# Attention by whole chunks, float32 scores in two row halves of the array, and equal slices of four chunks

## The chip, the cores and the metric

One core of a Trainium2 chip runs the whole program. The metric is the device time of one execution in microseconds. The engines of the core are TensorE (PE in the profile; its weight loads are PEld), VectorE (DVE), ScalarE (ACT), GpSimd (POOL) and SyncE (SP), which here only issues transfers.

## The reference

Two parts follow each other. A decaying linear attention over 4 batches, 8 heads, 768 positions and 64 features gives `x`; a feed-forward layer with a squared ReLU gives the output. Inputs of attention are float32; the weights of the layer are float64.

```python
for b in range(nb):                       # blocks of 64 positions
    intra = np.einsum('bhic,bhjc->bhij', qb, kb) * Dmask[None]     # lam^(i-j), zero above the diagonal
    intra = np.einsum('bhij,bhjd->bhid', intra, vb)
    inter = np.einsum('bhid,bhde->bhie', qb * lam_pow[None], kv_state)
    out[:, :, sl] = intra + inter
    kv_state = lam_block[None, :, None, None] * kv_state + np.einsum('bhsd,bhse->bhde', kb * rev_pow[None], vb)
...
x = out.transpose(0, 2, 1, 3).reshape(3072, 512)
h = x @ w_in                              # 512 x 2048
r = np.maximum(h, 0.0)
return ((r * r) @ w_out).astype(np.float32)   # 2048 x 512
```

## The kernel before, in words

**Attention.** It works in chunks of 128 positions: 6 chunks for each batch, 24 in all, numbered t. Heads go in pairs that fill the 128 partitions, 4 pairs for a chunk. For a pair, `scores` multiplies k by q, where q of the two heads is laid out block-diagonally (`qbd`, 128 rows, 256 columns), so that one product gives both heads. `masked` multiplies the scores by the powers of the decay (`mask`) on VectorE. `products` adds three kinds of products: what the chunk adds to the state (from k and v), the values (from v and the masked scores), and, where a chunk is not the first of its batch, the state times q. The first two kinds use column halves of the array, one for each head of a pair; the third uses the whole array. `update` brings the state `kv` up to date on VectorE. `prep` multiplies k and q by powers of the decay on GpSimd, in place.

**Two forms of the scores.** Up to chunk 8 they are float32 products. From chunk 9 on (`T1`), `divide` splits q and k into two parts each (`qh`, `ql`, `kh`, `kl`, type float32r), and `scores2` adds three products for each pair; `attend2` then takes two pairs at a time.

**Feed-forward.** It also keeps each operand in two float32r parts and leaves out the product of the two low parts. Tokens go in slices of 5, 4, 4, 4, 4 and 3 chunks (`GS`). In a slice, unit f of 16 computes 128 of the 2048 hidden features (`hidden`, 12 products of 512 columns for four chunks), `relu` and `square` on ScalarE (and VectorE) and `rest` on VectorE make the squares' two parts `gh` and `gl`, and `project` adds 3 products for each chunk to that chunk's bank. On TensorE the order is hidden(f), then attention for chunks of the next slice, then project(f-1). The split of the next slice's input, `xh` and `xl`, is done at the end of a slice from `xt`, since `xh` and `xl` exist once.

**Conversion of the weights.** A piece of 512 columns of float64 is turned into float32 bit by bit: `first` (two operations on ScalarE), `clamp`, `shift`, `sign`, `rounded` (VectorE), `upper` (ScalarE, the high part) and `lower` (VectorE, the low part; on GpSimd for pieces 0 and 2). There are 32 pieces, 16 for each matrix. Two are done before the first slice, and unit f of slice 0 converts two more. `wload` issues a piece's load when a buffer comes free.

**What sets the order.** Each engine runs its instructions in the order in which the program issues them. Tiles come from pools with a fixed number of buffers, and a new tile waits until the last user of its buffer is done. Transfers are issued on SP in program order as well; an instruction there that waits for a buffer holds up those behind it. PSUM has 8 banks: 4 for `project`'s sums (`ps_acc`), 2 for `hidden` (`ps_h`), one each for `ps_x` and `ps_a`.

**Start.** The decays' powers are computed on VectorE from `lam`, written to memory (`zd`) and read back as `mask` and `qpow`. Attention of the first five chunks runs before the feed-forward part, two pairs a step.

Of the kernel before, what the change touches and what calls it, by code (L numbers as in the profile page):

```python
# [9 lines left out]
I32 = mybir.dt.int32  # L10
# [16 lines left out]
GS = (5, 4, 4, 4, 4, 3)     # attention chunks in a slice of the feed-forward part  # L27
G0 = GS[0]
T1 = G0 + GS[1]             # from this chunk on, scores are products of operands in two parts
N = 4 * C  # L30
NM = len(GS)

NST, NA = 4, 4              # tiles for raw and converted weights
# [3 lines left out]
TURNS = [[1]] + [[j for j in (2 * f + 2, 2 * f + 1) if j < 2 * NF] for f in range(1, NF)]  # L37

# Before the first slice, step k takes two pairs of a chunk, and beside them:
CONVERT = (4, 5, 6, 7, 7)   # steps that convert piece 2 further  # L40
FIRST, RAW, SPREAD, LOW0, LOW2 = 3, 3, 2, 5, 8
AHEAD = {1: (5,), 2: (6,), 3: (7,), 4: (8,), 5: (9,)}   # steps whose scores it computes
LA = 10                     # pairs whose scores come before step 0
WARM = 2, 2
PARTS = 1, 2                # parts of a unit's first products that go before the scores
# [3 lines left out]
def body(ctx: ExitStack, tc: tile.TileContext, qT, kT, kvq, lam, w, out):  # L49
# [32 lines left out]
    warm(WARM[0])  # L82

    loaded, tok = {}, {}
    banks = [0]

    def bank():             # the banks of ps_acc and the one of ps_x in turn
        banks[0] += 1
        if banks[0] % G0 == 0:
            return ps_x.tile([P, DM], F32, name="x")  # L90
        return ps_acc.tile([P, DM], F32, name="acc")

    rooms = [const.tile([P, 3 * DM], F32, name=f"kvq{j}") for j in range(2)]

    def room(t):
        return rooms[t] if t < 2 else lent[:, 0 : 3 * DM] if t == 2 else rooms[(t + 1) % 2]

    def qroom(t):
        if t == G0 - 1 and t not in extra:
            extra[t] = wk.tile([P, DM], F32, name="q4", tag="A", bufs=NA)  # L100
        return extra[t] if t == G0 - 1 else room(t)[:, 2 * DM :]

    extra = {}

    def load_qk(t):
        if T1 <= t < NT:
            k_ = io.tile([P, NPR, C], F32, name="kT_sb", bufs=1)
            nc.sync.dma_start(out=k_, in_=kT[t])
            loaded[t] = None, k_
        elif t < NT:  # L110
            if t < G0 and t % 2:
                q_, k_ = qbd[1], lent[:, 3 * DM : 4 * DM].rearrange("p (a b) -> p a b", a=NPR)
            else:
                q_, k_ = qbd[0], io.tile([P, NPR, C], F32, name="kT_sb", bufs=1) if t != 2 else None
            if t == 2:
                k_ = wk.tile([P, DM], F32, name="k2", tag="A", bufs=NA).rearrange("p (a b) -> p a b", a=NPR)
            if t == 3:
                load_q(t)
            nc.sync.dma_start(out=k_, in_=kT[t])
            if t in (1, 2):  # L120
                load_q(t)
            elif t not in (3, 4):
                for j in range(2):
                    r = slice(j * D, (j + 1) * D)
                    nc.sync.dma_start(out=q_[r, :, j, :], in_=qT[t, r])
            loaded[t] = q_, k_

    def load_q(t):
        nc.sync.dma_start(out=qroom(t), in_=kvq[t, :, 2 * DM :])

    def spread(t):
        x = qroom(t).rearrange("p (a b) -> p a b", a=NPR)
        for j in range(2):
            r = slice(j * D, (j + 1) * D)
            nc.scalar.copy(loaded[t][0][r, :, j, :], x[r])

    def load_v(t):
        if t < NT:
            x = room(t)
            n = 3 * DM if t >= G0 and t % NCB or t >= T1 else 2 * DM  # L140
            nc.sync.dma_start(out=x[:, 0:n], in_=kvq[t, :, 0:n])
            x = x[:, 0:DM], x[:, DM : 2 * DM], qroom(t)
            tok[t] = [y.rearrange("p (a b) -> p a b", b=z) for y, z in zip(x, (D, D, C))]

# [1 line left out]
    wih = const.tile([P, NF, KT * P], F32R, name="wih")  # L146
    wil = const.tile([P, NF, KT * P], F32R, name="wil")
    woh = const.tile([P, NF, DM], F32R, name="woh")
    wol = const.tile([P, NF, DM], F32R, name="wol")
    NW = 2 * NF  # L150
    order = [0, 2] + [j for x in TURNS for j in x]
    raw, cv, loads = {}, {}, iter(order)

    def wload(n=1):
        for _ in range(n):
            j = next(loads, None)
            if j is not None:
                raw[j] = wk.tile([P, DM], I64, name="raw", tag="st", bufs=NST)
                nc.sync.dma_start(out=raw[j], in_=w[j % 2, :, j // 2])
# [5 lines left out]
    def first(j):  # L165
        r = raw.pop(j).bitcast(U32).rearrange("p (n two) -> p n two", two=2)
        A = wk.tile([P, DM], U32, name="A", bufs=NA)
        nc.scalar.activation(A.bitcast(F32), r[:, :, 1].bitcast(F32), AF.Abs)  # L168
        nc.scalar.activation(r[:, :, 0], r[:, :, 0], AF.Copy, scale=2.0**-29)
        cv[j] = r[:, :, 0], r[:, :, 1], A  # L170

    def clamp(j):           # beyond float32's range: to zero and to infinity
        A = cv[j][2].bitcast(F32)
        nc.vector.tensor_scalar(
            out=A, in0=A, scalar1=2.0**-15, scalar2=float(LIM), op0=ALU.max, op1=ALU.min
        )

    def shift(j):
        A = cv[j][2]
        nc.vector.tensor_scalar(  # L180
            out=A, in0=A, scalar1=3, scalar2=0x3FFFFFFF,
            op0=ALU.logical_shift_left, op1=ALU.bitwise_and,
        )

    def sign(j):
        L, Hw, A = cv[j]
        nc.vector.scalar_tensor_tensor(
            out=A, in0=Hw, scalar=0xC0000000, in1=A, op0=ALU.bitwise_and, op1=ALU.bitwise_or
        )

    def rounded(j):
        L, Hw, A = cv[j]
        nc.vector.tensor_tensor(out=A, in0=A, in1=L, op=ALU.add)
        if j not in order[:2]:
            wload()

    def upper(j):
        nc.scalar.copy((wih, woh)[j % 2][:, j // 2], cv[j][2].bitcast(F32))

    def lower(j, eng=nc.vector):  # L200
        hi, lo = ((wih, wil), (woh, wol))[j % 2]
        eng.tensor_tensor(  # L202
            out=lo[:, j // 2], in0=cv.pop(j)[2].bitcast(F32), in1=hi[:, j // 2].bitcast(F32),
            op=ALU.subtract,
        )
# [538 lines left out]
```

## Time and profile before

| | |
|---|---|
| time, median of 3 runs | 655.0 us (654.37 to 655.11) |
| span of the profiled execution | 653.3 us |
| TensorE busy | 642.7 us (98%) |
| VectorE busy | 342.1 us (52%) |
| ScalarE busy | 247.7 us (38%) |
| GpSimd busy | 55.0 us (8%) |
| moved by DMA | 50.41 MB, mean 77 GB/s |

The profiled execution's own time is given by its span; what lies around it (launch and end) is only in the times of the runs. Busy times are sums over one execution, and an engine's instructions are pipelined, so that a TensorE that is 98% busy isn't 98% used. A row such as `L454 PE MATMUL h<-xh,wih 128*128 128x512 f32 x256 | 69.1, 391` says: line 454, TensorE, result tile and operands, the part of the array that is used, the shape, how often, the busy time in us and the mean of one in ns. In rows with times, the first number is the start in us from the beginning of the span, the second the duration in us, and what stands in brackets is the idle time ahead of it and what ended it. In a table of stretches, the columns are the stretch and its length, then the busy time of PE, PEld, DVE, ACT and POOL, the granted clock of TensorE, the share of DMA and GB/s.

### The profile page before, as it was taken

The numbers are of one execution on the slowest core, as the hardware profiler recorded it, in microseconds if no ns is written. First come the engines' busy times: TensorE is split into PE (matmuls) and PEld (weight loads), VectorE is DVE, ScalarE is ACT, GpSimd is POOL, SyncE is SP. The second block draws the span as 40 slices with busy tenths as digits, with TensorE's granted clock in tenths as the row PEclk, the third lists the DMA queues.
The fourth block names the chain that finished last, engine by engine and source line by source line (L and its number), as shares of the span: only waits on it lengthen the run. The fifth ranks groups of instructions, "written<-read, shape, count | busy, mean of one in ns | idle before, by whom it ended". The sixth has DMA issues, their size and how long they took to land.

```text
span 653.3 us, 9153 instructions
## 1 busy us (share of the span) xinstructions
PE 642.7 (98%) x3620; PEld 533.3 (82%) x3620; DVE 342.1 (52%) x669; ACT 247.7 (38%) x459; POOL 55.0 (8%) x58
## 2 busy tenths in 40 slices
PE   7989999999999999999999999999999999999997
PEld 3778888888888888888888888788888888889996
DVE  4998887887743433735344454254474452242222
ACT  3367776676522232523313333223153222242222
POOL 2520101001101100101001010011010100000000
PEclk9899999999999999999999999999999999999999
DMA  6854545451420201211101121022031000010001
GB/s 230 301 178 140 203 147 189 132 212 45 145 64 1 65 23 42 82 49 64 65 1 65 33 97 64 1 65 66 1 128 49 19 0 1 0 65 1 0 2 48
DMA packets 19963, 50.41 MB, mean 77 GB/s; under 512 B 1992, under 2 KB 6096, under 8 KB 19920
## 3 DMA queue, kind: packets, MB, share of 16 engines
q1 hardware_dynamic: 19920, 49.82, 22.7%
q8 instruction: 28, 0.46, 0.3%
q14 instruction: 15, 0.12, 0.1%
HBM read 43.52 MB, written 6.30 MB: 76 GB/s over the span
## 4 chain that ended last, share of the span: by engine, by line
PE 92%; DVE 4%; DMA 3%; issue 1%; ACT 0%; SPq 0%; DVEq 0%
PE h L454 40%; PE acc L493 13%; PE acc L498 13%; PE acc L494 13%; PE x L414 3%; PE att L336 3%; PE att L331 3%; PE att L326 2%; DMA raw<-in_w 1%; DVE kv L369 1%; PE att L298 1%; DVE a L314 1%; DMA zd<-pw 1%; DMA mask<-zd 1%; PE x L493 1%
## 5 line engine op out<-in xcount | busy, mean ns | idle before, releaser
L463 ACT ACTIVATE r<-h 128x512 f32<-128x512 f32 (+2 forms) x112 | 59.6, 535 | 314.6 <-PE h L454 314.6
L472 DVE TENSOR_TENSOR r<-r 128x512 f32<-128x512 f32 (+1 forms) x80 | 60.2, 753 | 165.8 <-ACT gh L468 165.2
L493 PE MATMUL acc<-woh,gh 128*128 128x512 f32 x368 | 146.6, 398 | 0.0
L498 PE MATMUL acc<-woh,gl 128*128 128x512 f32 x368 | 143.9, 391 | 0.0
L494 PE MATMUL acc<-wol,gh 128*128 128x512 f32 x368 | 143.6, 390 | 0.0
L454 PE MATMUL h<-xh,wih 128*128 128x512 f32 (+2 forms) x448 | 110.1, 367 | 0.0
L454 PE MATMUL h<-xl,wih 128*128 128x512 f32 (+2 forms) x448 | 107.2, 360 | 0.3 <-DVE xl L555 0.3
L454 PE MATMUL h<-xh,wil 128*128 128x512 f32 (+2 forms) x448 | 106.1, 358 | 0.1
L454 PEld LDWEIGHTS h<-xl,wih 128*128 128x128 f32 x448 | 79.9, 188 | 11.0 <-DVE xl L555 0.5
L454 PEld LDWEIGHTS h<-xh,wil 128*128 128x128 f32 x448 | 79.4, 188 | 10.4 <-DVE wil L202 0.4
L454 PEld LDWEIGHTS h<-xh,wih 128*128 128x128 f32 x448 | 78.3, 188 | 10.2
L498 PEld LDWEIGHTS acc<-woh,gl 128*128 128x128 f32 x368 | 69.0, 188 | 15.3
L493 PEld LDWEIGHTS acc<-woh,gh 128*128 128x128 f32 x368 | 69.2, 188 | 13.7 <-ACT r L463 0.5
L494 PEld LDWEIGHTS acc<-wol,gh 128*128 128x128 f32 x368 | 69.2, 188 | 13.5
L477 DVE TENSOR_TENSOR gl<-r,gh 128x512 fp32r<-128x512 f32 (+2 forms) x96 | 69.1, 720 | 10.7 <-ACT r L470 4.2
L369 DVE SCALAR_TENSOR_TENSOR kv<-kv,qpow,att 64x64 f32<-64x64 f32 x96 | 26.9, 280 | 72.2 <-ACT xt L433 64.9
L468 ACT ACTIVATE gh<-r 128x512 fp32r<-128x512 f32 (+2 forms) x96 | 61.0, 635 | 1.7
L276 POOL TENSOR_TENSOR kvq<-kvq,qpow 128x512 f32<-128x512 f32 x17 | 22.0, 1291 | 413.7 <-DVE ql L404 327.4
L421 DVE TENSOR_TENSOR a<-x,mask 128x512 f32<-128x512 f32 x30 | 20.7, 690 | 13.4 <-PE x L414 13.0
L331 PE MATMUL att<-a,kvq 128*64 128x128 f32 x304 | 25.0, 277 | 0.0
L168 ACT ACTIVATE A<-raw 128x512 f32<-128x512 f32 x32 | 21.3, 666 | 8.2 <-DMA raw<-in_w 8.2
L336 PE MATMUL att<-kvq,kv 128*128 128x128 f32 x128 | 24.4, 305 | 0.0
(123 smaller groups left out, 582.2 us busy)
## 6 DMA issues: line engine op xcount, KB each, us to landing
raw<-in_w SPq DMA_DIRECT2D x32, 512.0 KB, 5.0
kvq<-in_kvq SPq DMA_DIRECT2D x18, 768.0 KB, 4.3
out_x<-o SPq DMA_DIRECT2D x24, 256.0 KB, 2.3
kT_sb<-in_kT SPq DMA_DIRECT2D x21, 256.0 KB, 2.6
kvq<-in_kvq SPq DMA_DIRECT2D x5, 512.0 KB, 5.3
qbd<-in_qT SPq DMA_DIRECT2D x10, 128.0 KB, 3.1
lent<-in_kT SPq DMA_DIRECT2D x2, 256.0 KB, 3.0
kvq<-in_kvq SPq DMA_DIRECT2D x2, 256.0 KB, 4.5
```

The costliest lines, as they stand in the source:

```text
L276: (nc.vector if t == 1 else nc.gpsimd).tensor_tensor(out=qd, in0=qd, in1=qpow, op=ALU.mult)
L331: nc.tensor.matmul(o[e][r], vs[:, 2 * p + j, :], a[:, 2 * e + j, :], start=e == 0 and clear, stop=not t % NCB, skip_group_check=True,)
L336: nc.tensor.matmul(o[e], kv[:, p, :], qd[:, p, :], start=False, stop=True, skip_group_check=True,)
L369: nc.vector.scalar_tensor_tensor(out=d, in0=d, scalar=qpow[r, p, C - 1 : C], in1=u[r], op0=ALU.mult, op1=ALU.add)
L454: nc.tensor.matmul(h, wt[:, f, kt * P : (kt + 1) * P], x[:, kt, cs], start=k == 0, stop=k == 11)
L463: nc.scalar.activation(rr, h, AF.Relu)
L468: nc.scalar.activation(gh, r, AF.Square)
L472: nc.vector.tensor_tensor(out=r, in0=r, in1=r, op=ALU.mult)
L477: nc.vector.tensor_tensor(out=gl, in0=r, in1=gh.bitcast(F32), op=ALU.subtract)
L493: nc.tensor.matmul(accs[m][i], gh[:, cs], woh[:, f], start=f == 0, stop=False)
L494: nc.tensor.matmul(accs[m][i], gh[:, cs], wol[:, f], start=False, stop=False)
L498: nc.tensor.matmul(accs[m][i], gl[:, cs], woh[:, f], start=False, stop=end)
```

## The change

It is a new version of the program's body. Constants and the computation of the powers stay; the arithmetic of the feed-forward part stays. What differs:

- All six slices have four chunks. Four chunks of attention run before the first slice.
- Attention takes a whole chunk at a time, one chunk for four units: scores in the first of them, `masked` in the second, `attend` in the third. Scores are float32 products throughout. Each head's product uses 64 rows of the array, the two heads of a pair the two row halves, and they write to two banks. `qbd`, `divide` and `scores2` are gone; `ps_a` has two banks and `ps_x` is gone.
- The state times q uses column halves as well, 8 products. The state's decay is multiplied ahead on GpSimd (`decay`, into `kvd`), and VectorE adds with two instructions for each chunk in place of eight.
- `xh` and `xl` have two buffers each; `attend` writes the next slice's input split into them, from the PSUM bank.
- Weights are converted in 17 lots: the first and the last are one piece, the others two (`pieces`), with one instruction of 1024 columns for each step. `lower` runs on GpSimd for all of them. Unit f of slice 0 converts lot f+2. `raw` and `A` have two buffers.
- `square` works in the PSUM bank: relu, and both squares on ScalarE. `rest` reads the bank.
- Loads: q and k of a chunk by features, and k and v by tokens, each in a tile with two buffers. Chunks 2 and 3 use memory of `xh` and `xl`. At the start the loads of four chunks and of lots 0 and 1 are issued in a row on SP; the transfers of the powers go by ScalarE's queue.
- The output is staged in tiles that use `raw`'s buffers.

The diff, cut to its core:

```diff
-GS = (5, 4, 4, 4, 4, 3)     # attention chunks in a slice of the feed-forward part
...
+G = 4
+N = G * C
+NM = NT // G
+NLOT = NF + 1
...
+    def load_qk(t):
+        if t in (2, 3):
+            lent[t] = wk.tile([P, 2, KT * C, 2], F32, name=f"lent{t}", tag=("xh", "xl")[t - 2])
+            x = lent[t][:, 0].rearrange("p a b -> p (a b)")
+        else:
+            x = io.tile([P, 2 * DM], F32, name="qk_sb")
...
+    def pieces(u):
+        return slice(max(2 * u - 1, 0), min(2 * u + 1, 2 * NF))
...
+            raw[u] = wk.tile([P, n], I64, name="raw", tag="raw")
...
+    def first(u):
+        if u < NLOT:
+            r = raw.pop(u).bitcast(U32).rearrange("p (n two) -> p n two", two=2)
+            A = wk.tile([P, r.shape[1]], U32, name="A")
+            nc.scalar.activation(A.bitcast(F32), r[:, :, 1].bitcast(F32), AF.Abs)
+            nc.scalar.activation(r[:, :, 0], r[:, :, 0], AF.Copy, scale=2.0**-29)
...
+    def lower(u, eng):
+        eng.tensor_tensor(
+            out=flat(wl, u), in0=cv.pop(u)[2].bitcast(F32), in1=flat(wh, u).bitcast(F32),
+            op=ALU.subtract,
+        )
...
+    wload(0)
+    load_kv(0)
+    load_qk(2)
+    load_kv(1)
+    load_kv(2)
+    wload(1)
+    load_qk(3)
+    load_kv(3)
...
+    def scores(t, pool, name):
+        sc_of[t] = [pool.tile([P, DM], F32, name=name) for _ in range(2)]
+        k_, q_ = feat[t][:, 0], feat[t][:, 1]
+        for p in range(NPR):
+            for j, r in enumerate(rows):
+                nc.tensor.matmul(
+                    sc_of[t][j][:, p * C : (p + 1) * C], k_[r, p], q_[r, p],
+                    start=True, stop=True, skip_group_check=True,
+                )
...
+    def attend(t, pool, name):
...
+        for p, j, r in heads if c else []:
+            nc.tensor.matmul(
+                o[r, p * C : (p + 1) * C], kv[:, p, rows[j]], q_[:, p, :], start=False, stop=True,
+                skip_group_check=True,
+            )
+        if c < NCB - 1:
+            for j, r in enumerate(rows):
+                x = u[r, 0 : NPR * D].rearrange("p (a b) -> p a b", a=NPR)
+                d = kv[r, :, rows[j]]
+                if c:
+                    V.tensor_tensor(out=d, in0=kvd[r], in1=x, op=ALU.add)
+                else:
+                    V.tensor_copy(d, x)
+        xh, xl = xs_of[t // G]
+        cs = slice(t % G * C, (t % G + 1) * C)
+        o = o.rearrange("p (a b) -> p a b", a=KT)
+        nc.scalar.copy(xh[:, :, cs], o)
+        return lambda: V.tensor_tensor(
+            out=xl[:, :, cs], in0=o, in1=xh[:, :, cs].bitcast(F32), op=ALU.subtract
+        )
+
+    def decay(t):
+        if t % NCB < NCB - 2:
+            for j, r in enumerate(rows):
+                nc.gpsimd.tensor_tensor(
+                    out=kvd[r], in0=kv[r, :, rows[j]],
+                    in1=qpow[r, :, C - 1 : C].broadcast_to([D, NPR, D]), op=ALU.mult,
+                )
...
+    def square(h):
+        nc.scalar.activation(h, h, AF.Relu)
+        gh = wk.tile([P, N], F32R, name="gh")
+        nc.scalar.activation(gh, h, AF.Square)
+        nc.scalar.activation(h, h, AF.Square)
+        return gh
...
+    first(0)
+    for op in (clamp, shift, sign, rounded):
+        op(0)
+    upper(0)
+    first(1)
+    prep_k(0)
+    masked(0)
+    prep_k(1)
+    prep_q(1)
+    later = [[], [clamp, shift], [sign], [rounded]]
+    for t in range(G):
+        if t + 1 < G:
+            masked(t + 1)
+        if t + 2 < G:
+            scores(t + 2, ps_acc, "acc")
+        low = attend(t, *((ps_h, "h") if t % 2 else (ps_a, "att")))
+        low()
+        decay(t)
+        if t + 2 < G:
+            prep_k(t + 2)
+            prep_q(t + 2)
+        for op in later[t]:
+            op(1)
+        if t == 1:
+            lower(0, nc.gpsimd)
+    upper(1)
+    lower(1, nc.gpsimd)
+    wload(2)
+    first(2)
...
     for m in range(NM):
+        if m + 1 < NM:
+            new_x(m + 1)
         for f in range(NF):
+            u = f + 2 if m == 0 and f + 2 < NLOT else None
+            t = (m + 1) * G + f // 4
+            step = f % 4 if t < NT else None
+            h = hidden(m, f, *xs_of[m])
+            if step == 1:
+                masked(t)
+            if u is not None:
+                wload(u + 1)
+                for op in (clamp, shift, sign):
+                    op(u)
+            gh = square(h)
+            low = attend(t, ps_a, "att") if step == 2 else None
+            if u is not None:
+                rounded(u)
+                upper(u)
+                first(u + 1)
+            rest(m, f, h, gh)
+            if low:
+                low()
+                decay(t)
+                if t + 2 < NT:
+                    load_qk(t + 2)
+                    load_kv(t + 2)
+            if u is not None:
+                lower(u, nc.gpsimd)
             if prev is not None:
                 project(*prev)
             prev = (m, f)
+            if step == 0:
+                scores(t, ps_a, "att")
+                prep_k(t)
+                prep_q(t)
```

More of the change, by code (lines that the diff above doesn't have):

```diff
@@ L26 @@
 NF = DF // P
-GS = (5, 4, 4, 4, 4, 3)
[L28 to L45, printed above, removed]
+G = 4
+N = G * C
+NM = NT // G
+NLOT = NF + 1
 @with_exitstack
@@ L80, in warm @@
             nc.tensor.matmul(w_, kv[:, 0, :], kv.rearrange("p a b -> p (a b)"), start=True, stop=True)
[L82 to L103, printed above, removed]
-    def load_qk(t):
[L106 to L143, printed above, removed]
@@ L146, in body @@
[L146 to L159, printed above, removed]
@@ L165, in first @@
[L165 to L176, printed above, removed]
@@ new lines, in w_out, with wload @@
+    def w_out(f):
+        return 2 * f + 2 if f < NF - 1 else 2 * NF - 1
+    def pieces(u):
+        return slice(max(2 * u - 1, 0), min(2 * u + 1, 2 * NF))
+    raw, cv = {}, {}
+    def wload(u):
+        if u < NLOT:
+            x = pieces(u)
+            n = (x.stop - x.start) * DM
+            raw[u] = wk.tile([P, n], I64, name="raw", tag="raw")
+            for i, j in enumerate(range(x.start, x.stop)):
+                of = (1, j // 2 - 1) if j and j % 2 == 0 else (1, NF - 1) if j == 2 * NF - 1 else (0, (j + 1) // 2)
+                nc.sync.dma_start(out=raw[u][:, i * DM : (i + 1) * DM], in_=w[of[0], :, of[1]])
@@ L183, in shift, with sign, rounded, flat @@
         )
-    def sign(j):
-        L, Hw, A = cv[j]
-        nc.vector.scalar_tensor_tensor(
+    def sign(u):
+        L, Hw, A = cv[u]
+        V.scalar_tensor_tensor(
             out=A, in0=Hw, scalar=0xC0000000, in1=A, op0=ALU.bitwise_and, op1=ALU.bitwise_or
         )
[L191 to L201, printed above, removed]
+    def rounded(u):
+        L, Hw, A = cv[u]
+        V.tensor_tensor(out=A, in0=A, in1=L, op=ALU.add)
+    def flat(t, u):
+        return t[:, pieces(u)].rearrange("p a b -> p (a b)")
+    def upper(u):
+        nc.scalar.copy(flat(wh, u), cv[u][2].bitcast(F32))
+    def lower(u, eng):
         eng.tensor_tensor(
-            out=lo[:, j // 2], in0=cv.pop(j)[2].bitcast(F32), in1=hi[:, j // 2].bitcast(F32),
+            out=flat(wl, u), in0=cv.pop(u)[2].bitcast(F32), in1=flat(wh, u).bitcast(F32),
             op=ALU.subtract,
@@ L426, in attend2 @@
-    def attend2(i, xt, at):
-        t, p0 = divmod(i, NPR)
-        c = t % NCB
-        b = ps_a.tile([P, DM], F32, name="att")
-        o = b[:, 2 * C :].rearrange("p (e i) -> p e i", e=2)
-        us = [b[:, e * D : (e + 1) * D] for e in range(2)] if c < NCB - 1 else None
-        products(t, (p0, p0 + 1), lot["a"], [o[:, 0], o[:, 1]], us, us is None)
-        nc.scalar.copy(xt[:, p0 : p0 + 2, at : at + C], o)
-        for e in range(2) if us else []:
-            update(i + e, us[e])
-    g_of, accs = {}, {}
@@ L440, in parts @@
-    def parts(m):
-        n = GS[m] * C
-        k = -(-n // 512)
-        return [slice(j * n // k, (j + 1) * n // k) for j in range(k)]
-    def hidden(m, f, xh, xl, todo):
-        r = one.tile([P, GS[m] * C], F32, name="r")
-        for cs in parts(m):
-            h = ps_h.tile([P, cs.stop - cs.start], F32, name="h")
-            todo.append((r, r[:, cs], h))
-            k = 0
-            for wt, x in ((wih, xh), (wih, xl), (wil, xh)):
-                for kt in range(KT):
-                    nc.tensor.matmul(
-                        h, wt[:, f, kt * P : (kt + 1) * P], x[:, kt, cs], start=k == 0, stop=k == 11
-                    )
-                    k += 1
-                    if k % 3 == 0:
-                        yield
@@ L482, in project @@
         if f == 0:
-            if m == 0:
-                accs[m] = []
-                for _ in range(G0):
-                    accs[m].insert(0 if (banks[0] + 1) % G0 == 0 else len(accs[m]), bank())
-            else:
-                accs[m] = [ps_acc.tile([P, DM], F32, name="acc") for _ in range(GS[m])]
+            accs[m] = [ps_acc.tile([P, DM], F32, name="acc") for _ in range(G)]
         end = f == NF - 1
+        j = w_out(f)
         def high(i):
             cs = slice(i * C, (i + 1) * C)
-            nc.tensor.matmul(accs[m][i], gh[:, cs], woh[:, f], start=f == 0, stop=False)
@@ L522, in body @@
-    for i in range(2 * NPR, LA):
-        scores(i)
-    warm(WARM[1])
+        xs_of[m] = [wk.tile([P, KT, N], F32R, name=n, tag=n) for n in ("xh", "xl")]
+    new_x(0)
+    scores(0, ps_acc, "acc")
+    scores(1, ps_acc, "acc")
+    warm(2)
     for h, n in ((0, 4), (4, 4)):
-        nc.sync.dma_start(
+        nc.scalar.dma_start(
             out=mask[:, h : h + n],
@@ L529, in body @@
         )
-    load_v(1)
     for j in range(2):
-        nc.sync.dma_start(
-            out=qpow[j * D : (j + 1) * D],
+        nc.scalar.dma_start(
+            out=qpow[rows[j]],
             in_=bass.AP(zd.tensor, zd.offset + j * Z + C, [[0, D], [2 * Z, NPR], [1, C]]),
         )
-    load_qk(3)
-    load_v(2)
-    load_q(4)
-    load_qk(4)
-    wload()
     first(0)
-    for op in (clamp, shift, sign):
+    for op in (clamp, shift, sign, rounded):
         op(0)
-    rounded(0)
+    upper(0)
@@ L545, in body @@
+    first(1)
+    prep_k(0)
     masked(0)
-    upper(0)
-    prep(0)
-    more = []
-    for op in (clamp, shift, sign, rounded, upper):
-        more.append(lambda op=op: op(2))
-    late = []
-    def xpart(o, p, cs):
-        nc.scalar.copy(xh[:, p, cs], o)
-        late.append(lambda: nc.vector.tensor_tensor(
-            out=xl[:, p, cs], in0=o, in1=xh[:, p, cs].bitcast(F32), op=ALU.subtract
-        ))
-    todo = []
-    early = hidden(0, 0, xh, xl, todo)
-    for k in range(NE // 2):
-        i = 2 * k
-        t, p = divmod(i, NPR)
-        masked(i + 2)
-        while late:
-            late.pop()()
-        for _ in range(CONVERT.count(k)):
-            more.pop(0)()
-        o, us = attend(i)
-        for e in range(2):
-            update(i + e, us[e])
-        if k == 1:
-            prep(1)
-        if t == G0 - 1:
-            next(early)
-            next(early)
-        for j in AHEAD.get(k, ()):
-            scores(2 * j)
-            scores(2 * j + 1)
-        cs = slice(t * C, (t + 1) * C)
-        if t == G0 - 1:
-            xpart(o, slice(p, p + 2), cs)
-        elif p == 2:
-            xpart(o_of.pop(t), slice(0, NPR), cs)
-        if p == 2:
-            t = (3, 4, NT, 5, 6)[t]
-            if t == 3:
-                spread(t)
-                prep(2)
-            load_v(t)
-            prep(t)
-        if k == RAW:
-            wload(2)
-        if k == SPREAD:
-            spread(4)
-        if k == FIRST:
-            first(2)
-        if k == LOW0:
-            lower(0, nc.gpsimd)
-        if k == LOW2:
-            lower(2, nc.gpsimd)
@@ L602, in body @@
-    for op in late + more:
-        op()
-    queue = iter(order[2:])
-    for j in TURNS[0]:
-        first(next(queue))
-    def split(kt):
-        nc.scalar.copy(xs[0][:, kt], xt[:, kt])
-        nc.vector.tensor_tensor(
-            out=xs[1][:, kt], in0=xt[:, kt], in1=xs[0][:, kt].bitcast(F32), op=ALU.subtract
-        )
+    prep_k(1)
[15 more added lines that the diff above has]
+        if t == 1:
+            lower(0, nc.gpsimd)
@@ L614, in body @@
+    upper(1)
+    lower(1, nc.gpsimd)
+    wload(2)
+    first(2)
+    for t in (4, 5):
+        load_qk(t)
+        load_kv(t)
     prev = None
[L615 to L616 removed]
     for m in range(NM):
[L618 removed]
+        if m + 1 < NM:
+            new_x(m + 1)
         for f in range(NF):
[L620 to L677 removed]
```

344 lines of the change are left out of this document (89 added, 255 removed).

## The prediction

> **What bounds the kernel now.** I read the page's head first, then busy time in four stretches that I cut where the work changes: attention alone, slice 0, slices 1 to 4, slice 5.
>
> ```profile
> span 653.3 us, 9153 instructions
> PE 642.7 (98%) x3620; PEld 533.3 (82%) x3620; DVE 342.1 (52%) x669; ACT 247.7 (38%) x459; POOL 55.0 (8%) x58
> ...
> 0.00:35.30 35.30, 29.36 (x219) 19.70 (x220) 25.75 (x88) 11.63 (x19) 13.83 (x22) 0.95 0.78 260
> 35.30:166.00 130.70, 130.24 (x800) 113.05 (x799) 107.72 (x222) 91.68 (x177) 10.31 (x11) 1.00 0.47 157
> 166.00:579.40 413.40, 413.38 (x2257) 337.89 (x2256) 187.51 (x324) 125.58 (x230) 30.84 (x25) 1.00 0.14 45
> 579.40:653.30 73.90, 69.76 (x349) 62.66 (x347) 21.16 (x37) 18.81 (x37) 0.00 (x0) 0.99 0.07 26
> ```
>
> TensorE is the bound from 35.3 us on: it has no idle time in slices 1 to 4. But in slice 0 VectorE is busy for 107.72 of 130.70 us and ScalarE for 91.68, because the weights are converted there. That slice has little room on three engines at once. The chain of waits, in order of time, gives the unit prices (start, us, what):
>
> ```profile
> 10.91 4.03 DMA mask<-zd
> ...
> 59.11 3.52 PE h L454 x24
> 67.29 3.52 PE h L454 x24
> ...
> 179.98 2.72 PE h L454 x12
> 185.42 0.71 PE x L414 x6
> ...
> 193.11 2.72 PE h L454 x12
> ...
> 557.69 2.72 PE h L454 x12
> 563.13 2.72 PE h L454 x12
> ...
> 648.03 0.45 PE acc L498 x2
> ```
>
> Starts of `hidden` 557.69 and 563.13: a unit of four chunks without attention is 5.44 us. 179.98 to 193.11: two units with two pairs' attention are 13.13, so attention for two pairs is 13.13 - 10.88 = 2.25: split scores 0.71, the rest 1.54. A whole chunk costs 4.50. In slice 0 a unit of five chunks with one pair takes 67.29 - 59.11 = 8.18. After TensorE's last matmul (648.48) 4.8 us of copy and store remain.
>
> **The change, part by part: TensorE.** All slices have four chunks: 96 units of 5.44 are 522.2 us, fixed. Attention: the starts of weight loads inside one `attend2` are
>
> ```profile
> 175.68 0.31 PEld L326 LDWEIGHTS att<-kvq 128*64 128x64 f32 x8 [0.35 <-issue]
> 175.91 0.42 PEld L331 LDWEIGHTS att<-a,kvq 128*64 128x64 f32 x8
> 176.50 0.52 PEld L336 LDWEIGHTS att<-kvq,kv 128*128 128x128 f32 x4 [0.17 <-issue]
> L326 PEld LDWEIGHTS att<-kvq 128*64 128x64 f32 x240 | 9.9, 136 | 10.8 <-issue 10.2 <-POOL kvq L281 0.2 <-DVE A L180 0.2
> ```
>
> Each float32 product is two instructions. The array waits 0.35 where it goes from the whole array to column halves and 0.17 on the way back. A chunk at once has the products of two `attend2`, 3.08, less one entry (0.35) and, as the state's products now use column halves too, both returns (0.34): 2.4. The scores become 8 products on 64 rows each, 16 instructions, alternating between the row halves and two banks. No row shows row halves. Nearest is L331: 8 instructions of 128 columns in column halves, 0.42. Twice that is 0.85, plus entry 0.35 and exit 0.1: 1.3. Chunks that start a batch lack the state's products and those that end one the update (mean of -0.1 to -0.2). I take 3.6 per chunk where it was 4.5. Ends: 3.2 (no entry waits) and 4.45 (row halves one after the other, +0.85). Sixteen chunks stand beside slices 1 to 4: 57.6 us.
>
> Whether the weight loads allow this: eight loads of 64 columns span 0.31 with 136 ns for one, so they start 25 ns apart; sixteen of 128 columns would need 0.8, no more than the products. The Trainium skill, "TensorE: Matmul & The Clock Gate", section "LDWEIGHTS (loading the stationary operand)", counts columns over 1.2 per ns, and not rows, so a 64-row load saves nothing: by it sixteen loads take 1.71 us, and the sum would be 13.7 us higher. The eight loads above took less than that rule gives (0.43), so I do not follow it.
>
> **Conversion in slice 0.** Two pieces become one operation of 1024 columns, and `lower` moves from VectorE to GpSimd for all of them. Within a round everything is one ring: `upper(u)`, then `first(u+1)` behind it on ScalarE, then clamp, shift, sign and rounded on VectorE, then `upper(u+1)`. Before, two pieces were interleaved on each engine, and the ring hid under 8.18 us of TensorE. Its parts at 512 columns, and how they grow:
>
> ```profile
> 10.74 0.67 ACT L168 ACTIVATE A<-raw 128x512 f32<-128x512 f32 x1
> 11.45 0.43 DVE L174 TENSOR_SCALAR A<-A 128x512 f32<-128x512 f32 x1 [4.84 <-ACT A L168]
> 11.91 0.43 DVE L180 TENSOR_SCALAR A<-A 128x512 uint32<-128x512 uint32 x1
> 12.37 0.69 DVE L187 SCALAR_TENSOR_TENSOR A<-raw,A 128x512 uint32<-128x512 uint32 x1
> 13.21 0.69 DVE L193 CUSTOM_DVE_ANT_0 A<-raw,A 128x1024 uint16<-128x1024 uint16 x1
> 13.93 0.62 ACT L198 CAST wih<-A 128x512 fp32r<-128x512 f32 x1 [1.93 <-DVE A L193]
> L477 DVE TENSOR_TENSOR gl<-r,gh 128x640 fp32r<-128x640 f32 x16 | 13.2, 822 | 4.6 <-ACT r L470 4.2
> L477 DVE TENSOR_TENSOR gl<-r,gh 128x384 fp32r<-128x384 f32 x16 | 8.9, 559 | 1.6
> L468 ACT ACTIVATE gh<-r 128x640 fp32r<-128x640 f32 x16 | 11.9, 746 | 0.0
> L468 ACT ACTIVATE gh<-r 128x384 fp32r<-128x384 f32 x16 | 8.4, 526 | 0.5
> L202 POOL TENSOR_TENSOR wil<-A,wih 128x512 fp32r<-128x512 f32 x2 | 2.8, 1375 | 0.0
> L281 POOL TENSOR_TENSOR kvq<-kvq,mask 128x128 f32<-128x128 f32 x4 | 1.5, 402 | 11.5 <-DMA mask<-zd 11.5
> L281 POOL TENSOR_TENSOR kvq<-kvq,mask 128x512 f32<-128x512 f32 x18 | 20.9, 1162 | 4.8 <-DMA kvq<-in_kvq 4.8
> ```
>
> VectorE adds (822-559)/256 = 1.03 ns per column, half that in clamp and shift (next fence), ScalarE 0.86, GpSimd (1162-402)/384 = 1.98. At 1024 columns: upper 1.06, Abs 1.11, clamp 0.74, shift 0.74, sign 1.37, rounded 1.25 and two hand-overs of 0.04: 6.35 us. TensorE's mean in slice 0 is 5.44 + 3.6/4 = 6.34. So the ring would just not matter, if nothing held it. But `lower` on GpSimd runs right after `upper`, when clamp is next. What a GpSimd operation does to VectorE:
>
> ```profile
> 25.53 1.06 POOL L281 TENSOR_TENSOR kvq<-kvq,mask 128x512 f32<-128x512 f32 x1 [2.03 <-DMA kvq<-in_kvq]
> 25.57 0.68 DVE L555 TENSOR_TENSOR xl<-acc,xh 128x512 fp32r<-128x512 f32 x1
> 26.17 0.70 DVE L174 TENSOR_SCALAR A<-A 128x512 f32<-128x512 f32 x1
> 26.55 1.45 POOL L276 TENSOR_TENSOR q<-q,qpow 128x512 f32<-128x512 f32 x1
> ...
> 509.34 1.06 POOL L281 TENSOR_TENSOR kvq<-kvq,mask 128x512 f32<-128x512 f32 x1
> 509.71 1.24 DVE L472 TENSOR_TENSOR r<-r 128x512 f32<-128x512 f32 x1 [1.84 <-ACT gh L468]
> ```
>
> The clamp that began at 26.17 ended at 26.87, 0.28 after GpSimd's operation (26.59); the product at 509.71 ended at 510.95, 0.55 after GpSimd's (510.40). Both waited for its end. The subtraction at 25.57, which reads a PSUM bank and one SBUF operand, lost nothing. The Trainium skill, "SBUF — State Buffer", section "Who interferes with whom", says the same of a pair of ports that one instruction holds to its end; by that rule a 1024-column `lower` holds it throughout, which no row here shows at that length.
>
> `lower` at 1024 columns: 1.375 + 512 x 1.98 ns = 2.4 us (ends: 2.0, and 2.75 for twice the row). It starts 1.14 after `rounded` and ends at 3.53; clamp, which would have ended at 1.06+1.11+0.08+0.74 = 2.99, ends at 3.53+0.55 = 4.08. The ring becomes 6.35+1.1 = 7.4 us (6.35 with no hold, 7.8 at the upper end). Fourteen rounds are 103.6; the last piece, half as wide, 5.8.
>
> Attention adds to this ring. The state's addition (two of 64x256, 0.43 each by the slope) stands ahead of `rounded` in three of four chunks: 2.5. `prep_k` (1.06) and `prep_q` (some 1.2) hold the ports while clamp and shift wait: three of each, less the overlap at the hand-over, 5.6. `decay` 0.3 three times. Together 9. `masked` fits into VectorE's wait for Abs and costs nothing; if that cover went, 1.4 a chunk. So from `rounded(1)` to `rounded(16)`: 118 us; 96 with no hold, 125 at the upper end. TensorE follows it: `project(f)` needs `rest(f)`, which is behind `rounded(f+2)` on VectorE.
>
> **Startup.** `rounded(1)` starts that count. The loads ahead of it, four chunks (4 MB) and three pieces (1.5), are issued at once; mask and powers (0.75) go by ScalarE's queue. In binary MB that is 6.55e6 bytes. The best stretch before is
>
> ```profile
> 16.30:32.60 16.30, 16.30 (x170) 12.27 (x168) 15.55 (x40) 5.48 (x9) 9.80 (x9) 0.90 0.89 301
> ```
>
> 301 GB/s: all is there near 24 us, lot 1 of the weights, 5.5e6 bytes deep, near 21. `first(1)` stands on ScalarE ahead of the copy of chunk 0: 21 + 2.2 + 0.6 = 23.8. Then VectorE in order: `xl` 0.7, three chunks of masks (1.38), state (0.85) and `xl` (0.68), 8.7, lot 1's four operations 4.1, GpSimd's holds 0.7: `rounded(1)` at 38. The mask itself, at 15 before (10.91 + 4.03), may come by 17 and hides. Bounds: 33 (loads no limit) and 43 (mask late, clock low after the idle array).
>
> **The sum.** 38 + 118; then `rest` 0.75 and what is left of a projection, 3.0; one projection 2.72; 80 units 435.2; attention 57.6; tail 4.8: 503.3. Span 659.3, against 653.3. The median shown, 655.0, lies 1.7 above the span: 661.0 us. At no cost: output staging in the raw weights' buffers (free after slice 0), and the second input buffer, since the split at a slice's end never stopped TensorE in slices 1 to 4 (uncovered, the last chunk's copy and subtraction would be 1.3 a slice). The second square moves to ScalarE: three operations of 0.64 by the slope and `rest`, 2.6 us, under the 5.44 until `project` needs them; 2.6 a unit if that cover went. `wload(u+1)` waits on SP for `rounded(u-1)`, behind a chunk's loads that wait for `attend(t)` in one unit of four, and has a round plus 1 us to land: hidden unless 1 MB needs over 8.4.
>
> **Rivals.** (1) The other side: `lower` does not hold up the ring (VectorE gets the ports first, or the hold is short). Then TensorE bounds slice 0: it begins by 36, 522.2, 20 chunks of 3.6, 3 for the first units' late weights, tail 4.8: 638, so 639.7 us. It decides where the round falls to 6.34. For: 6.35 without the hold. Against: both waits above. (2) Row halves take turns: 0.85 x 16 = 13.6 on top, 674.6. In slice 0 it would hide. For: column halves are all the trace shows. Against: loads 25 ns apart. (3) The raw lots come late: 1 us a round is 14 us, 675. For: 1 MB per round beside 1 MB of a chunk. Against: 157 GB/s already in slice 0, 301 possible.
>
> **How the numbers follow.** Forecast 0.55, its own range 651 to 670 (ring 7.05 to 7.8, startup ±4); rival 1 0.25; rival 2 0.12; rival 3 0.08. Faster by over 0.2% (about what a measurement of this kernel can tell from none) is rival 1 and the forecast's low end, 0.31; within it, 653.7 to 656.3, 0.08; slower 0.61. Range 640 to 673: below it half of rival 1's lower tail, above it most of rivals 2 and 3.
>
> **What would show it.** Rounds of 7.2 to 7.8 us between the 2048-wide additions of slice 0, a clamp that ends 0.55 after each `lower`; slice 0's end, where units of slice 1 begin, near 159 us against 166; quads of units in slices 1 to 4 at 25.2 against 26.26. Scores' 16 instructions in 0.85: right; 1.7: rival 2. Wrong if clamp never waits, if rounds are at 6.4, or if `rounded(1)` is outside 33 to 43.

## The result, and the profile after

The changed kernel takes 665.8 us (median of 4 runs, 664.83 to 666.52), the one before 655.06 in the same comparison: a ratio of 1.0163, 95% interval 1.0148 to 1.0177. It is slower by 1.6%. Forecast were 661.0 us, and a range, 640 to 673, that holds the measured time. The profiled execution's span is 664.7 us.

The page's head, and the busy time by stretches (cut at the startup's end, slice 0's, slice 4's; columns as before):

```profile
span 664.7 us, 8862 instructions
PE 624.6 (94%) x3720; PEld 505.0 (76%) x3720; DVE 226.4 (34%) x324; ACT 230.0 (35%) x376; POOL 111.5 (17%) x98
```

```profile
0.00:40.00 40.00, 22.41 (x248) 16.87 (x248) 19.82 (x62) 7.53 (x10) 15.72 (x24) 0.83 0.72 244
40.00:160.00 120.00, 102.32 (x586) 78.64 (x586) 100.49 (x94) 71.35 (x94) 49.85 (x27) 0.99 0.47 154
160.00:576.00 416.00, 415.17 (x2514) 339.72 (x2515) 93.06 (x151) 124.55 (x225) 45.90 (x49) 1.00 0.14 46
```

TensorE has 18 us less to do in all, yet in slice 0 it is busy for only 102.32 of 120 us, where before it had no gap. VectorE's total fell from 342.1 to 226.4 us, but in slice 0 it is busy for 100.49 of 120. The unit that begins slice 1 starts at 163.2 us; before it was 166.0, but that slice was one of five chunks and five chunks' attention had run ahead of it. What is now done later is one chunk's share of 16 units (5.44 / 4 = 1.36 us each) and one chunk of attention (3.9, see below): 16 x 1.36 + 3.9 = 25.7 us. At equal work the new kernel stands at 188.9, so startup and slice 0 cost 22.9 us more, and the rest (475.8 against 487.3) 11.5 less. The difference is the 11.4 us between the spans.

One plain round of slice 0 (a round is the conversion of one lot; a plain one has nothing of the attention in it), on VectorE, then ScalarE, then GpSimd (start, us):

```profile
73.33 1.23 DVE L139 CUSTOM_DVE_ANT_0 A<-raw,A 128x2048 uint16<-128x2048 uint16 x1
74.47 0.68 DVE L325 TENSOR_TENSOR gl<-h,gh 128x512 fp32r<-128x512 f32 x1
76.69 1.98 DVE L122 TENSOR_SCALAR A<-A 128x1024 f32<-128x1024 f32 x1 [1.54 <-ACT A L116]
78.71 0.69 DVE L126 TENSOR_SCALAR A<-A 128x1024 uint32<-128x1024 uint32 x1
79.44 1.23 DVE L133 SCALAR_TENSOR_TENSOR A<-raw,A 128x1024 uint32<-128x1024 uint32 x1
80.80 1.23 DVE L139 CUSTOM_DVE_ANT_0 A<-raw,A 128x2048 uint16<-128x2048 uint16 x1
```

```profile
74.59 1.05 ACT L145 CAST wh<-A 128x1024 fp32r<-128x1024 f32 x1 [2.76 <-DVE A L139]
75.54 1.12 ACT L116 ACTIVATE A<-raw 128x1024 f32<-128x1024 f32 x1
```

```profile
75.71 2.41 POOL L148 TENSOR_TENSOR wl<-A,wh 128x1024 fp32r<-128x1024 f32 x1 [5.06 <-ACT wh L145]
```

`rounded` to `rounded` is 80.80 - 73.33 = 7.47 us. The clamp on VectorE lasts 1.98 us, where the same shape next to it (`shift`) takes 0.69; it ends at 78.67, 0.55 after GpSimd's `lower` (78.12). And TensorE waits for what VectorE does at the end of a round, `rest`, in fourteen units (by the waits: us in total, times, longest):

```profile
PE acc L342 <- DVE gl L325: 18.1, 14, 2.6
```

The units of slice 1, on TensorE, at their first products (the four units around one whole chunk):

```profile
209.12 1.07 PE L310 MATMUL h<-xh,wh 128*128 128x512 f32 x4
214.56 1.07 PE L310 MATMUL h<-xh,wh 128*128 128x512 f32 x4
220.09 1.16 PE L224 MATMUL att<-qk_sb 64*128 64x128 f32 x16
221.19 1.19 PE L310 MATMUL h<-xh,wh 128*128 128x512 f32 x4
226.76 1.07 PE L310 MATMUL h<-xh,wh 128*128 128x512 f32 x4
234.79 1.07 PE L310 MATMUL h<-xh,wh 128*128 128x512 f32 x4
245.76 1.16 PE L224 MATMUL att<-qk_sb 64*128 64x128 f32 x16
270.96 1.16 PE L224 MATMUL att<-qk_sb 64*128 64x128 f32 x16
295.75 1.16 PE L224 MATMUL att<-qk_sb 64*128 64x128 f32 x16
```

A plain unit is 5.44; the scores add 1.19 to their unit and 0.13 to the next, `attend` 8.03 - 5.44 = 2.59: 3.9 for a whole chunk. From scores to scores it is 25.67 with a whole chunk, 25.20 and 24.79 where a batch ends or begins. Before, 26.26.

The startup, from the chain, then TensorE, then ScalarE with its queue (ACTq) and the copy of the first chunk's attention, then the first and the last `rounded` of the ring of rounds:

```profile
11.57 9.55 DMA mask<-zd
```

```profile
22.00 2.67 PE L224 MATMUL acc<-lent 64*128 64x128 f32 x16 [12.18 <-DVE a L247]
```

```profile
12.13 3.56 ACTq L374 DMA_DIRECT2D qpow<-zd  x2
15.72 1.28 ACT L116 ACT_TABLE_LOAD   x1 [15.72 <-DMA mask<-zd]
27.47 0.58 ACT L289 CAST xh<-att 128x512 fp32r<-128x512 f32 x1 [4.59 <-PE att L269]
```

```profile
40.89 1.37 DVE L139 CUSTOM_DVE_ANT_0 A<-raw,A 128x2048 uint16<-128x2048 uint16 x1
159.30 0.76 DVE L139 CUSTOM_DVE_ANT_0 A<-raw,A 128x1024 uint16<-128x1024 uint16 x1
```

The mask takes 9.55 us to land (4.03 before) and comes at 21.1. TensorE stands idle for 12.18 us ahead of the third chunk's scores, and these sixteen instructions then take 2.67 us, where the same sixteen take 1.16 in slice 1; the granted clock is 0.50 from 15 to 25 us. ScalarE is held by the issue of the powers' transfer until 15.72. `rounded(1)` ends at 42.26, `rounded(16)` at 160.06.

### The profile page after: what moved, and what is told of

Same layout as the page of the kernel before. It is cut to its first block, busy times and chain, and to the rows that moved or that the text cites. A ratio compares the mean times of both kernels' runs of the same rounds, so it can differ in the third digit from the quotient of the medians.

```text
span 664.7 us, 8862 instructions
## 1 busy us (share of the span) xinstructions
PE 624.6 (94%) x3720; PEld 505.0 (76%) x3720; DVE 226.4 (34%) x324; ACT 230.0 (35%) x376; POOL 111.5 (17%) x98
## 4 chain that ended last, share of the span: by engine, by line
PE 77%; DVE 13%; DMA 4%; issue 2%; ACT 2%; POOL 1%; SPq 0%; ACTq 0%; DVEq 0%; POOLq 0%
PE h L310 33%; PE acc L337 12%; PE acc L342 11%; PE acc L338 11%; DVE A L122 4%; DVE A L139 3%; DVE A L133 3%; PE att L224 3%; PE att L269 2%; ACT A L116 2%; PE att L274 2%; DVE A L126 2%; DMA mask<-zd 1%; PE att L264 1%; DMA qk_sb<-in_qT 1%
## 5 line engine op out<-in xcount | busy, mean ns | idle before, releaser
L317 ACT ACTIVATE h<-h 128x512 f32<-128x512 f32 x96 | 55.9, 583 | 336.0 <-PE h L310 336.0
L342 PE MATMUL acc<-wh,gl 128*128 128x512 f32 x384 | 151.6, 396 | 18.1 <-DVE gl L325 18.1
L337 PE MATMUL acc<-wh,gh 128*128 128x512 f32 x384 | 152.3, 397 | 0.0
L338 PE MATMUL acc<-wl,gh 128*128 128x512 f32 x384 | 150.2, 391 | 0.0
L310 PE MATMUL h<-xh,wh 128*128 128x512 f32 x384 | 105.4, 396 | 1.9 <-DVE kv L283 1.9
L310 PE MATMUL h<-xl,wh 128*128 128x512 f32 x384 | 102.9, 390 | 0.0
L310 PE MATMUL h<-xh,wl 128*128 128x512 f32 x384 | 102.6, 389 | 0.0
L342 PEld LDWEIGHTS acc<-wh,gl 128*128 128x128 f32 x384 | 72.4, 188 | 39.3 <-DVE gl L325 24.5
L337 PEld LDWEIGHTS acc<-wh,gh 128*128 128x128 f32 x384 | 72.4, 188 | 17.4 <-issue 2.6
L338 PEld LDWEIGHTS acc<-wl,gh 128*128 128x128 f32 x384 | 72.4, 189 | 14.5
L320 ACT ACTIVATE h<-h 128x512 f32<-128x512 f32 x96 | 57.0, 594 | 0.0
```

Source lines behind the costliest of these rows:

```text
L310: nc.tensor.matmul(h, wt[:, w_in(f), kt * P : (kt + 1) * P], x[:, kt], start=k == 0, stop=k == 11)
L317: nc.scalar.activation(h, h, AF.Relu)
L320: nc.scalar.activation(h, h, AF.Square)
L337: nc.tensor.matmul(accs[m][i], gh[:, cs], wh[:, j], start=f == 0, stop=False)
L338: nc.tensor.matmul(accs[m][i], gh[:, cs], wl[:, j], start=False, stop=False)
L342: nc.tensor.matmul(accs[m][i], gl[:, cs], wh[:, j], start=False, stop=end)
```

## Experiments

All times are medians, the ratios against the kernel before with 95% intervals. "Ring" is the time from the end of `rounded(1)` to that of `rounded(16)`, 117.8 us in the changed kernel.

**Is it GpSimd's hold that sets slice 0?** Two kernels, one without `lower` on GpSimd in the rounds, one with it twice.

```diff
-                lower(u, nc.gpsimd)
+                lower(u, nc.vector)
```

> In slice 0, lower runs on VectorE, in the same place of the program; the startup's two stay on GpSimd. Hold theory (GpSimd's 2.4 us operation keeps clamp waiting): the clamp falls from 1.98 to 0.7 us; VectorE gets 1.24 us more work, most of it in its wait for the next Abs; a plain round falls from 7.47 to about 6.3, rounded(1) to rounded(16) from 118 to about 104, the time from 666 to about 652. Ring theory without a hold (the ring is as long whoever does lower): rounds stay at 7.4 or grow by lower's 1.2 us on VectorE, time 666 to 683.

Measured: 652.87 us, ratio 0.9966 (0.9956 to 0.9977): faster than the kernel before, and 12.9 us below the changed one. The ring is 104.9. A round on VectorE (with `xl` of a chunk in it; the one after it, without, takes 6.29):

```profile
90.94 1.23 DVE L139 CUSTOM_DVE_ANT_0 A<-raw,A 128x2048 uint16<-128x2048 uint16 x1
92.08 0.68 DVE L325 TENSOR_TENSOR gl<-h,gh 128x512 fp32r<-128x512 f32 x1
92.68 0.68 DVE L290 TENSOR_TENSOR xl<-att,xh 128x512 fp32r<-128x512 f32 x1
93.28 1.23 DVE L148 TENSOR_TENSOR wl<-A,wh 128x1024 fp32r<-128x1024 f32 x1
94.42 0.69 DVE L122 TENSOR_SCALAR A<-A 128x1024 f32<-128x1024 f32 x1
95.15 0.69 DVE L126 TENSOR_SCALAR A<-A 128x1024 uint32<-128x1024 uint32 x1
95.88 1.22 DVE L133 SCALAR_TENSOR_TENSOR A<-raw,A 128x1024 uint32<-128x1024 uint32 x1
97.24 1.23 DVE L139 CUSTOM_DVE_ANT_0 A<-raw,A 128x2048 uint16<-128x2048 uint16 x1
```

The clamp takes 0.69 and the round 6.30 us, although VectorE has one operation of 1.23 us more to do. Nothing else in the program was touched.

```diff
+                x = cv[u]
+                lower(u, nc.gpsimd)
+                cv[u] = x
                 lower(u, nc.gpsimd)
```

> In slice 0, lower runs twice on GpSimd, with the same result: GpSimd's time doubles, no other engine has more to do. Hold theory: the second one holds the ports again while shift waits, 2.4 us more less what fell to the first wait's slack, rounds about 9.8, time about 666 + 14 x 2.4 = 700. Without a hold: GpSimd has 5 us of work in a round of 7.5, so nothing changes, 666.

Measured: 693.69 us, ratio 1.0586 (1.0569 to 1.0604). The direction and most of the size are the hold's; the price was over-estimated: a plain round is 9.53, 2.06 more than 7.47, and not 2.4 more. VectorE and GpSimd show why:

```profile
81.47 1.97 DVE L122 TENSOR_SCALAR A<-A 128x1024 f32<-128x1024 f32 x1 [1.54 <-ACT A L116]
83.47 2.76 DVE L126 TENSOR_SCALAR A<-A 128x1024 uint32<-128x1024 uint32 x1
```

```profile
80.49 5.19 POOL L148 TENSOR_TENSOR wl<-A,wh 128x1024 fp32r<-128x1024 f32 x2 [4.33 <-ACT wh L145]
```

The clamp gets in between the two subtractions (it ends at 83.44, GpSimd goes on to 85.68), and the shift then waits for the second and ends 0.55 after it. A hold lasts for the instruction, and what waits is let in at its end. The Trainium skill, "SBUF — State Buffer", section "Who interferes with whom", says that the first to issue has the shared ports for the whole instruction and that the other is blocked, not slowed; both traces agree, with a clamp of 1.98 and 1.97 us against 0.69.

**Do row halves of the array work side by side?** Both heads' scores on the first 64 rows (the second head's scores are left out; the count and shape of the products stay).

```diff
-                    sc_of[t][j][:, p * C : (p + 1) * C], k_[r, p], q_[r, p],
+                    sc_of[t][j][:, p * C : (p + 1) * C], k_[rows[0], p], q_[rows[0], p],
```

> Leaves out the second head's scores: both products of a pair use the first 64 rows, so both run in the same row half of the array; number, size and banks of the products stay. If row halves run side by side, a chunk's 16 instructions take 0.85 us more in slices 1 to 4: 16 chunks, 13.6 us, time about 679. If they already took turns, nothing changes, 666.

Measured: 683.46 us, ratio 1.0441 (1.0419 to 1.0463). TensorE:

```profile
199.84 2.05 PE L224 MATMUL att<-qk_sb 64*128 64x128 f32 x16
```

2.05 against 1.16 us for sixteen instructions on alternating halves: the halves do overlap, and alternating them saves 0.89 a chunk, 14.2 us over slices 1 to 4. The first of these instructions, on one half and then on alternating halves, in windows of 0.2 us, and after them the weight loads of all sixteen in the same order:

```profile
199.84 0.37 PE L224 MATMUL att<-qk_sb 64*128 64x128 f32 x1
220.09 0.38 PE L224 MATMUL att<-qk_sb 64*128 64x128 f32 x2
199.83 1.86 PEld L224 LDWEIGHTS att<-qk_sb 64*128 64x128 f32 x16 [0.35 <-issue]
220.09 0.97 PEld L224 LDWEIGHTS att<-qk_sb 64*128 64x128 f32 x16 [0.35 <-issue]
```

Two instructions on the two halves take 0.38 us together, where one takes 0.37: they start as a pair. The loads of the two halves overlap as well. The other 4.5 of the 18.7 us between the spans are in the startup, where `rounded(1)` ends at 46.73; the ring stays at 117.8, so slice 0 hides the scores' price, as the second rival said. The Trainium skill, "TensorE: Matmul & The Clock Gate", section "Part 3: Packing small matmuls — row/col tiling", says that a weight load overlaps running products only where the row group differs. These rows do not show that condition: on one half, too, the loads (1.86 us busy) lie beside the products (2.05). What they show is that loads of different halves overlap each other, at 0.97 us busy against 1.86.

**Can the ring be shortened on ScalarE?** The next lot's absolute value ahead of `upper`, with `lower` on GpSimd, and on VectorE.

```diff
-                upper(u)
                 first(u + 1)
+                upper(u)
```

> first(u+1) is issued ahead of upper(u) on ScalarE, so that Abs and scale of the next lot do not wait for this lot's rounding; lower stays on GpSimd. Ring theory: clamp no longer waits for ScalarE, it starts after rest, 0.7 after rounded; lower's hold then falls on shift. Rounds about 6.8, time about 657. If the next lot's load lands later than that (it is issued when rounded(u-1) is done), rounds stay above 7 and ScalarE shows waits for raw.

Measured: 660.95 us, ratio 1.0089 (1.0071 to 1.0106); the ring is 112.9, 4.9 shorter, and a plain round down to 6.73. About half of the expected gain: ScalarE's absolute value now waits 28.7 us for raw loads, in 13 places, the condition that the expectation named. With `lower` on VectorE as well:

> Both edits: lower on VectorE and first(u+1) ahead of upper(u). VectorE then has 5.4 us of conversion and rest in a round plus 0.7 of attention, 6.1, and TensorE 6.4: TensorE bounds slice 0, rounds about 6.4, rounded(1) to rounded(16) about 96, time about 645. If loads of the raw lots are the limit beneath, rounds stay at 7 or more, time 655 or above.

Measured: 656.6 us, ratio 1.0028 (1.0012 to 1.0044): slower than with `lower` alone, and a clear miss; the ring is 108.3. The waits of ScalarE, and ScalarE itself:

```profile
ACT A L116 <- DMA raw<-in_w: 27.2, 14, 2.7
```

```profile
64.31 1.17 ACT L116 ACTIVATE A<-raw 128x1024 f32<-128x1024 f32 x1 [2.72 <-DMA raw<-in_w]
65.36 1.15 ACT L117 ACTIVATE raw<-raw 128x1024 uint32<-128x1024 uint32 x1
66.39 1.04 ACT L145 CAST wh<-A 128x1024 fp32r<-128x1024 f32 x1
```

Two things were missed. A lot's load is issued when `rounded` of two lots earlier is done, and now ScalarE stands waiting for it in all fourteen rounds, with `upper` queued behind: here `rounded` ended at 65.36 and `upper` starts at 66.39. In the changed kernel and with `lower` alone on VectorE, ScalarE has no such wait in the rounds. And a plain round was at 6.3 already by another path: with `lower` ahead of the clamp on VectorE, it goes `rounded`, `upper`, `lower`, clamp, shift, sign, and the absolute value isn't on it, though only by a little: in the round shown for `lower` on VectorE it ends at 94.30, and the clamp starts behind `lower` at 94.42. So the early order could save next to nothing and cost 3.4 us of ring. Whether a third buffer for the raw weights would cure the first was not tried.

**How much is the startup worth?** The mask's and the powers' transfers on SP, ahead of what is loaded for later.

```diff
-    load_kv(2)
-    wload(1)
-    load_qk(3)
-    load_kv(3)
...
-        nc.scalar.dma_start(
+        nc.sync.dma_start(
...
+    load_kv(2)
+    wload(1)
+    load_qk(3)
+    load_kv(3)
```

> The mask and the powers are loaded by SP, ahead of the loads of chunk 2's k and v, lot 1 and chunk 3, which are issued after them. Startup theory (the mask's 9.55 us beside the other loads, and ScalarE held in issuing the powers until 15.7): the mask lands near 15, rounded(1) falls from 42.3 to 37 to 39, time to about 662. If the sum of all loads is the limit, lot 1 and chunk 3 come as much later as the mask comes earlier, and rounded(1) stays at 41 to 43, time 666.

Measured: 663.01 us, ratio 1.012 (1.0102 to 1.0138): 2.8 us below the changed kernel. The mask is there when VectorE first uses it at 16.19 (21.25 in the changed kernel), `rounded(1)` ends at 39.71, 2.55 earlier. Part of that may be scatter: in the four other kernels whose startup is that of the changed one, the profiled executions have it at 40.99 to 41.82. And the edit does two things at once: it puts the mask ahead of later loads, and it takes the issue of the powers off ScalarE. Which of them brings the gain was not separated. Now lot 1's load is late, and the first chunk's copy stands behind it on ScalarE:

```profile
21.83 1.12 ACT L116 ACTIVATE A<-raw 128x1024 f32<-128x1024 f32 x1 [9.37 <-DMA raw<-in_w]
22.84 1.13 ACT L117 ACTIVATE raw<-raw 128x1024 uint32<-128x1024 uint32 x1
23.86 0.58 ACT L285 CAST xh<-att 128x512 fp32r<-128x512 f32 x1
```

All three edits together:

> Mask first, lower on VectorE and first(u+1) ahead of upper(u). If startup and slice 0 add up: 666 - 21 - 4 = 641. If the earlier start only moves the wait to the loads of lots 2 and 3, as in the mask-first kernel alone, 645.

Measured: 655.8 us, ratio 1.0009 (0.9995 to 1.0022), no change that can be told from none. The miss is that of the early order: ScalarE waits 37.8 us for raw loads in 16 places. Without the early order, then:

> Subtraction on VectorE in slice 0 (the one that brought 652.87) and the mask's transfers ahead of the third and fourth chunks' loads on SP's queue (the change that brought 2.8 us by itself and put the second lot's rounding 2.55 us earlier). If the subtraction and the startup are separate terms of one sum: 652.9 - 2.8 = 650. If the lots' loads now set the ring's pace, as they did when the copies were asked for early, the startup's gain is given back: 653, with idle time of ScalarE's absolute value ended by raw's DMA in some of the fourteen rounds.

Measured: 650.71 us, ratio 0.9933 (0.9918 to 0.9949): the two gains add up. With `first(1)` behind the first chunk's copy:

```diff
-    first(1)
...
         low = attend(t, *((ps_h, "h") if t % 2 else (ps_a, "att")))
+        if t == 0:
+            first(1)
```

> The same, and lot 1's first copies on ScalarE behind the first chunk's hi copy of the attention instead of ahead of it. That copy stood behind a raw load that ended at 21.8 us and came at 23.9; the chunk after it then starts up to 2 us earlier. Sum of terms: 649 (1 us less than without it, since the second lot's rounding in turn waits for the copies now behind). If the second lot's rounding is the startup's end and not the chunks, no change to the kernel without it: 650.

Measured: 649.63 us, ratio 0.9913 (0.99 to 0.9926). `rounded(1)` starts at 36.11 against 36.17, so its place is the same and the 1 us between the medians, whose intervals meet, is not shown to be this edit's. And the subtractions of the startup on VectorE too:

> The same, and the subtractions of lots 0 and 1 on VectorE too, which GpSimd still does with the subtraction of slice 0 moved. There the first round took 9.35 us against 6.30 of a plain one, its clamp 1.98, its sign 2.20. Theory of the GpSimd hold: the first round falls to about 7.5, so 1.5 to 2 us less: 647. Rival, that the rounds' loads set the pace: the second lot's rounding is no longer what the third waits for, and the time stays at 649.

Measured: 649.36 us, ratio 0.9911 (0.9898 to 0.9924), the same. The first theory was right on its round and wrong on the sum. VectorE in this kernel, then in the one without the edit:

```profile
30.48 1.75 DVE L148 TENSOR_TENSOR wl<-A,wh 128x512 fp32r<-128x512 f32 x1
38.26 1.32 DVE L139 CUSTOM_DVE_ANT_0 A<-raw,A 128x2048 uint16<-128x2048 uint16 x1
45.62 1.23 DVE L139 CUSTOM_DVE_ANT_0 A<-raw,A 128x2048 uint16<-128x2048 uint16 x1
```

```profile
36.11 1.37 DVE L139 CUSTOM_DVE_ANT_0 A<-raw,A 128x2048 uint16<-128x2048 uint16 x1
45.48 1.23 DVE L139 CUSTOM_DVE_ANT_0 A<-raw,A 128x2048 uint16<-128x2048 uint16 x1
```

The first round falls from 9.37 to 7.36 us, but lot 0's subtraction, 1.75 us on VectorE, stands ahead of the last chunks' attention, and `rounded(1)` starts 2.15 later. The next rounding is where it was (45.62 against 45.48), and the time with it.

## Why the prediction was right

- **The ring** was the deciding step, and it held: 117.8 us against 118, a plain round 7.47 against 7.4, `lower` 2.41 against 2.4, the clamp's end 0.55 after it. That the sum is right to 0.2 us is partly luck: fourteen plain rounds are 104.6 where 103.6 was taken, and attention adds 7.5 (117.8 - 104.6 - 5.7 for the last round without its state addition) where 9 was taken. The slope for clamp and shift, half of 1.03 ns a column, can't be read in the fence that the prediction points at, which has one length only; the changed kernel's rows bear it out (0.43 us at 512 columns, 0.69 at 1024). That GpSimd's hold is the cause is shown from both sides, by the kernel without it (ring 104.9, time 652.9) and the one with two (693.7).
- **TensorE's part**, everything after `rounded(16)`: 664.7 - 160.06 = 504.6 against 503.3. The term that was short is attention: 3.9 for a whole chunk and 3.7 in the mean of sixteen (two at 3.03, three at 3.44, eleven at 3.9), where 3.6 was taken, 1.7 us in all. The tail was 0.8 shorter (4.0 us after the last product, where 4.8 was taken), and the other terms are 0.4 longer. Scores were right (1.32 against 1.3); `attend` is 2.59, not 2.4. From the price of two separate steps the prediction took off an entry of 0.35, which is idle time of the weight loads; the products lose less there: the first of `attend` starts 0.99 us after the first of the last four of `hidden` (229.57 - 228.58), and four such products take 0.91.
- **The startup** is the term that was mis-sized: `rounded(1)` at 42.26, near the upper bound of 43, where 38 was taken. The step that failed is "the mask itself, at 15 before, may come by 17 and hides". It came at 21.1, beside the loads issued in a row. The bound named the reason, a late mask and a low clock, and both are in the trace. The loads themselves were no limit: lot 1's copies on ScalarE were done at 22.88. But the first chunk's copy behind them waited 4.59 us for TensorE and ended at 28.05, where 23.8 was forecast. That is all of the 4.3 us; from there to `rounded(1)` it is 14.2, as forecast. So slice 1 begins at 163.2, and not near 159. The experiment with the mask first brings 2.8 us of time; how the 4.3 us divide between the mask's transfer and the low clock was not taken apart.
- 1.3 of TensorE's part and 4.3 of startup, less 0.2 of ring, are the 5.4 us by which the span exceeds the 659.3 of the sum; 0.6 us lower stands the offset of the median above the span (1.1 for 1.7).
- **Rivals.** The first (no hold) is refuted in the changed kernel, but its mechanism is what one edit brings about; its price, 639.7, would still be too low, as far as the nearest kernel shows: with `lower` on VectorE and rounds of 6.30 the ring is 104.9, since the attention's chunks add to it. The second (row halves take turns) is refuted by the kernel on one half. The third (raw loads late) is absent in the changed kernel and appears as soon as the copies are asked for earlier.

## What to carry to other kernels

Work that moves from VectorE to GpSimd isn't off VectorE's path when an operation there then waits for GpSimd's end: look in the trace for one that takes a multiple of its own time and ends a fixed bit after GpSimd's. In a ring of hand-overs between engines, add up the path of one round with every queue it passes, and again after each edit: a second path of almost the same length, or the load behind it, takes over. A transfer that starts last and is needed first belongs ahead of the loads for later work, on a queue where nothing stands behind its issue.

## What the hardware showed unexpectedly

- VectorE is let in between two GpSimd operations that follow each other directly: a waiting clamp ended at 83.44 us, with GpSimd busy from 80.49 to 85.68. The two took 5.19 us, 0.37 more than twice 2.41.
- The same mask transfer took 9.55 us beside the startup's loads, issued on ScalarE's queue, and 4.03 before, on SP's; the runs do not separate the loads from the queue. The issue of the powers' two transfers held ScalarE's queue for 3.56 us; on SP's queue, ahead of the later loads, it took 1.33.
- The first products after scores on row halves are slower too: the next four of `hidden` took 1.19 us where they take 1.07 elsewhere, and their unit 0.13 more.
